# Conversions issued one operation at a time, the fold on one half of w_out at a time, and keys and queries loaded without a second copy

## The chip, the cores and the metric

The kernel runs on one core of one Trainium2 chip. The metric is the time of one execution on the device in microseconds (us). Three runs of the kernel before took 1641.61, 1646.22 and 1648.20 us, so the median is 1646.22. Five engines work side by side: TensorE (PE in the profile; its weight loads are shown as PEld), VectorE (DVE), ScalarE (ACT), GpSimd (POOL) and SyncE (SP), which here issues every DMA.

## The reference

The reference is an attention block followed by a gated network, all in float32; the network's weights arrive as float64.

```
scores = scale * q @ k^T                       # 8 batches, 12 heads, 448 rows, head size 64
scores = einsum('bhij,hg->bgij', scores, w_pre)  # mixes the 12 heads
attn   = softmax(scores - max)                 # over the 448 keys
attn   = einsum('bhij,hg->bgij', attn, w_post)
x      = attn @ v, written as 3584 tokens of 768
out    = ((x @ w1) * (x @ w2)) @ w3 @ w_out    # 768 -> 1024 -> 1024 -> 768
```

## The kernel before, in words

**Precision.** A float32 product is made of three faster products: each operand is split into a high part and a low part, and high x high, high x low and low x high are summed in one PSUM bank. The splitting is a CAST on ACT (or DVE) for the high part and a subtraction on POOL (or DVE) for the low part.

**Steps.** The attention is cut into 360 steps of ten query rows (45 per batch), each with all 12 heads. The loop in `run` writes the instructions of all engines step by step, and each engine works through its list in order; no scheduler moves anything. For step n the list holds: the fetch of the raw scores of step n+4 (`r`), the exponential with its minimum (`softmax(n)`: `mn` on DVE, `e` on ACT), the row sums and scaled weights of step n-1 (`scale`: `sa`, `ri`, `w` on DVE), the split of the scores of step n+2 (`split_r`: `rh`, `rl`), the product with `w_post` for step n-2 (`post`: `pso` on PE, copied to `mt` on ACT), and at the end the mix by `w_pre` of step n+1 (`mix`: three matmuls into `psm`). Every 15 steps come the products with v (`av`: `psa`, 48 matmuls in two of the steps). A mix is the mark of a step's end in what follows.

**Raw scores.** The raw scores of a batch go to DRAM (`raw_d`) before they are fetched in blocks of ten rows. For batch 0 they are made in full float32 from `kqz` (`qk_first`, `psz`): two heads at a time, one on the upper 64 rows of the array, one on the lower 64. For batches 1 to 7 they are made by `qk`, one unit per head and quarter of the rows, 7 x 48 = 336 units. The head's 64 rows of queries sit twice in a 128-row tile, and the keys' high part and low part share one 128-row tile `kk`. One matmul with the queries' high part (L193) gives high x high + high x low, and one with the low part (L194) gives the rest. Both contract over 128 rows. `load_kq` brings a pair of heads as three blocks of 448 columns: each head's queries twice over the partitions, and the keys once. `split_kq` makes `qh`, `ql` and `kk` from them.

**Weights.** Each float64 weight is read as two int32 words and made float32 by a conversion: a square on ACT (`cm`, L102) and four DVE operations (`ca` three times, `cx` once, L112 to L116) for a piece of up to 384 columns; then the piece is split. 40 pieces belong to w3 and w_out: `folding` multiplies w3 and w_out into one matrix w34 ahead of time (`psf`, L352), 384 matmuls in all, called atoms here. It walks over eight columns f of w3 and two halves of w_out. 32 pieces belong to w1 and w2. Before step 50 (`SWITCH`) the background work of TensorE is the fold; afterwards it is the network (`eg`, `eo` for batch 0, `e..` for the other batches in pairs, with seven products in place of eight). How many background atoms a step gets is set by a table `share`, which gives more to steps with less other matmul work. A step takes one whole piece, if there is one and the step has no product with v.

Of the kernel before, what the change touches and what calls it, by code (L numbers as in the profile page):

```python
# [17 lines left out]
HP = H // 2  # L18
# [27 lines left out]
class Kernel:  # L46
# [52 lines left out]
    def square(self, s, name):  # L99
        n = s.shape[1]  # L100
        m = self.cx.tile([128, CW], F32, tag="m", name=f"cm{name}", bufs=1)[:, :n]
        self.nc.scalar.activation(m, s[:, :, 1].bitcast(F32), AF.Square)  # L102
        return m

    def to_f32(self, s, m, name):


        nc, n = self.nc, s.shape[1]
        low, top = s[:, :, 0], s[:, :, 1]

        a = self.bank(5, f"ca{name}").bitcast(I32)[:, :n]
        nc.vector.tensor_scalar(a, top, 3, 0x3FFFFFFF, op0=ALU.logical_shift_left, op1=ALU.bitwise_and)  # L112
        nc.vector.scalar_tensor_tensor(a, top, -0x40000000, a, op0=ALU.bitwise_and, op1=ALU.bitwise_or)
        nc.vector.scalar_tensor_tensor(a, low, 29, a, op0=ALU.logical_shift_right, op1=ALU.bitwise_or)
        x = self.cx.tile([128, CW], F32, tag="x", name=f"cx{name}")[:, :n]
        nc.vector.scalar_tensor_tensor(x, m, TINY2, a.bitcast(F32), op0=ALU.is_ge, op1=ALU.mult)  # L116
        return x
# [5 lines left out]

    def converting(self, jobs):

        words, made = [], None
        jobs = list(jobs)
        for n in range(-2, len(jobs) + 1):  # L130
            if n + 2 < len(jobs):
                src = jobs[n + 2][0]
                words.append(self.words(src, f"{self.n_words}"))
                self.n_words += 1
            if made:
                jobs[n - 1][1](made)
                made = None
            if 0 <= n < len(jobs):
                s = words.pop(0)
                m = self.square(s, f"{self.n_made}")  # L140
            yield
            if 0 <= n < len(jobs):
                made = self.to_f32(s, m, f"{self.n_made}")
                self.n_made += 1
            yield
# [24 lines left out]
    def load_kq(self, b, p):  # L170
        t = self.kp.tile([128, 3, S], F32, tag="kq", name=f"kq{b}_{p}")
        self.nc.sync.dma_start(t, self.kq[b, p])
        self.kqs[b, p] = t

    def split_kq(self, b, h, q_lo, k_lo):
        nc, t, s = self.nc, self.kqs[b, h // 2], h % 2
        qh = self.kp.tile([128, S], F32R, tag="qh", name=f"qh{b}_{h}")
        ql = self.kp.tile([128, S], F32R, tag="ql", name=f"ql{b}_{h}")
        kk = self.kp.tile([128, S], F32R, tag="kk", name=f"kk{b}_{h}")
        a, z = slice(s * D, (s + 1) * D), slice((1 - s) * D, (2 - s) * D)  # L180
        nc.scalar.copy(qh, t[:, s])  # L181
        nc.scalar.copy(kk[a], t[a, 2])
        q_lo.tensor_tensor(ql, t[:, s], qh.bitcast(F32), op=ALU.subtract)  # L183
        k_lo.tensor_tensor(kk[z], t[a, 2], kk[a].bitcast(F32), op=ALU.subtract)
        self.parts[b, h] = (qh, ql, kk)

    def qk(self, b, h, c, i, copy):
# [6 lines left out]
        nc.tensor.matmul(p, ql[:, cols], kk, start=False, stop=True)  # L194
# [126 lines left out]
    def fold_jobs(self):  # L321
# [4 lines left out]
        yield from columns[0]  # L326
        for q in range(2):
            for k in range(KF):
# [3 lines left out]
        for f in range(1, KF):  # L332
            yield from columns[f]
# [6 lines left out]
    def folding(self):  # L340
        nc = self.nc
        for f in range(KF):
            for half in range(2):
                w = self.fw[f]

                i = 1 if f == half == 0 else 6 + half
                p = self.bank(i, f"psf{half}_{f}")[:, :DH]
                atoms = [(k, t, x, y) for k in range(KF) for t, (x, y) in enumerate(PAIRS)]
                for k, t, x, y in atoms:
                    if (k, t) != (0, 0):  # L350
                        yield
                    nc.tensor.matmul(p, w[:, k, x], self.fo[:, k, y, half * DH:(half + 1) * DH],  # L352
                                     start=(k == 0 and t == 0), stop=(k == KF - 1 and t == 2))
                z = self.fp.tile([128, 3, 2, 128], F32R, tag="z", name=f"fz{half}_{f}")
                q = p.rearrange("p (d c) -> p d c", c=128)
                dst = self.w34_d[half * 3:(half + 1) * 3, :, f].rearrange("d p t c -> p d (t c)")

                def low(z=z, q=q, dst=dst):
                    nc.vector.tensor_tensor(z[:, :, 1], q, z[:, :, 0].bitcast(F32), op=ALU.subtract)
                    self.later.append(lambda: nc.sync.dma_start(dst, z.rearrange("p d t c -> p d (t c)").bitcast(F32)))  # L360

                self.ends.append((i, lambda z=z, q=q: nc.scalar.copy(z[:, :, 0], q)))
                self.soon.append((i, low))
                yield
# [368 lines left out]
    def run(self):  # L733
# [20 lines left out]
        self.cs, self.n_words, self.n_made = self.pool("cs", 2), 0, 0  # L754
# [16 lines left out]
        fold_pieces = self.converting(self.fold_jobs())  # L771
        next(fold_pieces)
        next(fold_pieces)
        next(fold_pieces)
        next(fold_pieces)
# [10 lines left out]
        next(fold_pieces)  # L786
        next(fold_pieces)
# [26 lines left out]
        FOLD, SWITCH, E_AT = 18, NB + 5, NB + 8  # L814
# [34 lines left out]
        def there(p):  # L849

            f, r = divmod(p - 3 - 2 * KF, 3)
            return 2 * KF * 3 * (1 + f) + (0, 9, 18)[r] if f >= 0 else min(max(3 * (p - 3), 0), KF * 3)

        wanted, LF, turn = 0, 4, itertools.chain((6, 7, 0) * 9, itertools.cycle((6, 7)))
# [8 lines left out]
        next(fold_pieces)  # L863
        next(fold_pieces)
        held()
        next(fold_pieces)
        next(fold_pieces)
# [7 lines left out]
        self.unit_list = self.units()  # L875
        self.n_one, self.w_made = len(self.unit_list), 4 * KF
        self.unit_list += self.pair_units()
        unit_pieces, phases = self.converting(self.unit_jobs()), list(self.phases())
        nq, n_pieces = 0, -2
        for n in range(N + 6):  # L880
# [4 lines left out]
            if n == SWITCH:  # L885
# [5 lines left out]
                assert not fold_pieces  # L891
# [9 lines left out]
            if n == PAIR:  # L901

                assert done >= 2 * E_1 + E_2 and unit_pieces is None and not self.jobs and not self.ys
# [22 lines left out]

            p, pieces = self.n_made - 1 if fold_pieces else 2 * KF + 3 * KF, None
            if avs.get(n):
                pass
            elif fold_pieces:  # L930
                f = (self.n_made - 1 - 2 * KF) // 3
                if f < 2 or done >= 2 * KF * 3 * (f - 1):
                    pieces = fold_pieces
                    if next(pieces, self) is self:
                        fold_pieces = pieces = None
# [9 lines left out]
            for x in qks.get(n, []):  # L945
                store = self.qk(*x, nq % 2, nc.scalar.copy)
                nq += 1
                if store:
# [97 lines left out]
```

## Time and profile before

| | |
|---|---|
| three runs, median | 1641.61 to 1648.20 us, 1646.22 us |
| the profiled execution, its span | 1641.97 us, 1640.2 us |
| PE busy, DVE busy, ACT busy, POOL busy | 96%, 63%, 61%, 67% of the span |
| DMA | 446.10 MB, mean 272 GB/s |
| raw-score units (L193 and L194) | 336 pairs of matmuls |
| split of queries and keys (L181 to L184) | 84 of each |

The rows of the groups give the line, the engine, the operation, what is written from what, how many there are, the busy time and the mean duration of one, then the idle time of the engine just before them. A matmul row has the rows and columns of the array that it uses (128*112 is 128 rows by 112 columns). Matmuls overlap with the next one, so a matmul's duration is longer than the distance between two starts; the distance between starts is what a matmul takes of the engine.

### The profile page before, as it was taken

What the parts mean: (1) busy time and instruction counts of PE and PEld (TensorE: products, weight loads), DVE (VectorE), ACT (ScalarE), POOL (GpSimd) and SP (SyncE); (2) the same over time, 40 slices, a digit from 0 to 9 for tenths busy, and PEclk for the clock granted to TensorE, in tenths of its full rate; (3) what the DMA queues carried; (4) which work ended last, traced back from release to release, by engine and by line L of the source; (5) the groups of instructions that cost most, each with busy time, mean ns of one, the idle gap of its engine ahead of it and who ended that gap; (6) DMA issues with size and microseconds to landing.
All of it is one profiled execution on the core that took longest, in us unless ns stands there. A gap on an engine that the chain in (4) does not pass through costs nothing. (4 is left out here: it accounts for less than half of the span.)

```text
span 1640.2 us, 31803 instructions
## 1 busy us (share of the span) xinstructions
PE 1580.9 (96%) x10548; PEld 1419.6 (87%) x10548; DVE 1037.3 (63%) x2304; ACT 996.3 (61%) x2413; POOL 1098.8 (67%) x940
## 2 busy tenths in 40 slices
PE   6979999999999999999999999999999999999999
PEld 2569997888898888889899898899899898999988
DVE  5957767788757777863465565745555557634573
ACT  4867666677766676776666666666665554542321
POOL 3766555676657788884676776876675666655774
PEclk7989999999999999999999999999999999999999
DMA  8989779998899999999978977889988866779875
GB/s 264 320 258 284 240 238 295 286 310 274 277 268 305 317 335 329 323 345 304 318 242 268 294 242 238 260 269 304 308 254 245 241 190 195 215 220 308 284 234 180
DMA packets 233906, 446.10 MB, mean 272 GB/s; under 512 B 21838, under 2 KB 159054, under 8 KB 233678
## 3 DMA queue, kind: packets, MB, share of 16 engines
q1 hardware_dynamic: 233742, 444.08, 85.5%
q8 instruction: 83, 1.36, 0.4%
q14 instruction: 81, 0.66, 0.1%
HBM read 309.90 MB, written 134.09 MB: 271 GB/s over the span
## 5 line engine op out<-in xcount | busy, mean ns | idle before, releaser
L221 POOL TENSOR_TENSOR rl<-r,rh 120x448 fp32r<-120x448 f32 x360 | 447.4, 1243 | 326.5 <-DVE rh L220 108.6
L237 DVE TENSOR_REDUCE mn<-psm 120x1 f32<-120x448 f32 x360 | 223.9, 622 | 405.0 <-PE psm L230 403.7
L240 ACT ACTIVATE e<-psm,mn 120x448 f32<-120x448 f32 x360 | 228.0, 633 | 346.9 <-DVE sa L249 295.2
L263 PEld LDWEIGHTS pso<-w,e 120*112 120x112 f32 (+1 forms) x2880 | 346.3, 177 | 47.2 <-ACT mt L269 33.8
L263 PE MATMUL pso<-w,e 120*112 120x120 f32 (+1 forms) x2880 | 359.7, 268 | 18.9 <-ACT mt L269 18.5
L694 PE MATMUL e<-eh,wu 128*128 128x448 f32 x1008 | 304.0, 371 | 1.1 <-DVE c L648 1.1
L269 ACT COPY mt<-pso 112x480 f32<-112x480 f32 x360 | 206.6, 574 | 13.3 <-PE pso L263 8.5
L694 PEld LDWEIGHTS e<-eh,wu 128*128 128x128 f32 x1008 | 187.3, 188 | 15.6 <-DVE c L648 1.9
L220 DVE CAST rh<-r 120x448 fp32r<-120x448 f32 x342 | 193.9, 567 | 7.5 <-DMA r<-raw_d 7.1
L198 ACT COPY st<-psq 112x448 f32<-112x448 f32 x336 | 173.0, 526 | 30.4 <-DMA raw_d<-st 26.1
L694 PE MATMUL e<-el,wu 128*128 128x448 f32 x504 | 187.2, 372 | 2.4 <-POOL el L633 2.2
L294 PE MATMUL psa<-mt,v 112*64 112x150 f32 (+1 forms) x2304 | 157.5, 293 | 1.9 <-DMA v<-v 1.9
L183 POOL TENSOR_TENSOR ql<-kq,qh 128x448 fp32r<-128x448 f32 x84 | 98.7, 1175 | 80.3 <-ACT qh L181 79.9
L294 PEld LDWEIGHTS psa<-mt,v 112*64 112x64 f32 x2304 | 144.2, 137 | 8.3 <-DMA v<-v 2.3
L228 PE MATMUL psm<-rh,wph 120*120 120x448 f32 x360 | 139.1, 386 | 9.2 <-DVE rh L220 9.2
L648 DVE TENSOR_TENSOR c<-c,e 128x448 f32<-128x448 f32 x168 | 101.2, 615 | 68.4 <-PE e L694 64.1
L230 PE MATMUL psm<-rl,wph 120*120 120x448 f32 x360 | 132.6, 368 | 0.6 <-POOL rl L221 0.5
L229 PE MATMUL psm<-rh,wpl 120*120 120x448 f32 x360 | 132.4, 368 | 0.0
L193 PE MATMUL psq<-kk,qh 128*112 128x448 f32 x336 | 124.8, 372 | 7.7 <-ACT st L198 7.5
L514 PE MATMUL eg<-xh,wu 128*128 128x448 f32 x384 | 128.1, 383 | 0.0
L194 PE MATMUL psq<-kk,ql 128*112 128x448 f32 x336 | 123.2, 367 | 0.0
L633 POOL TENSOR_TENSOR el<-x,eh 128x448 fp32r<-128x448 f32 x90 | 105.6, 1194 | 9.1 <-DMA x<-x_d 5.4
(113 smaller groups left out, 2958.8 us busy)
## 6 DMA issues: line engine op xcount, KB each, us to landing
r<-raw_d SPq DMA_DIRECT2D x352, 210.0 KB, 4.3
raw_d<-st SPq DMA_DIRECT2D x168, 392.0 KB, 4.8
wu<-w_d SPq DMA_DIRECT2D x104, 384.0 KB, 5.7
wu<-s_d SPq DMA_DIRECT2D x96, 384.0 KB, 4.4
v<-v SPq DMA_DIRECT2D x144, 224.0 KB, 4.9
kq<-kq SPq DMA_DIRECT2D x42, 672.0 KB, 7.1
wu<-w_d SPq DMA_DIRECT2D x51, 512.0 KB, 5.9
wu<-s_d SPq DMA_DIRECT2D x36, 512.0 KB, 4.4
```

The costliest lines, as they stand in the source:

```text
L198: copy(st[:, c % 2], p)
L220: (nc.gpsimd if 1 < n < SCORES else nc.vector).tensor_copy(rh[:K], r[:K])
L221: nc.gpsimd.tensor_tensor(rl[:K], r[:K], rh[:K].bitcast(F32), op=ALU.subtract)
L228: nc.tensor.matmul(p[:K, :S], self.wph[:K, :K], rh[:K], start=True, stop=False)
L229: nc.tensor.matmul(p[:K, :S], self.wpl[:K, :K], rh[:K], start=False, stop=False)
L230: nc.tensor.matmul(p[:K, :S], self.wph[:K, :K], rl[:K], start=False, stop=True)
L237: nc.vector.tensor_reduce(mn[:K], p[:K, :S], axis=AX.X, op=ALU.min)
L240: nc.scalar.activation(e[:K], p[:K, :S], AF.Exp, bias=mn[:K], scale=-1.0, accum_out=sm[:K])
L263: nc.tensor.matmul(p[:, j, :, :w], e[:K, j * JT:(j + 1) * JT], w2[:K, :, :w], start=True, stop=True)
L269: self.ends.append((4, lambda: copy(dst, p[:, :, :, :w])))
L294: nc.tensor.matmul(self.psa[rows, g % 3, :W], v[:, j, rows], mt[:, j, 2 * g + s, :W], start=(j == 0), stop=(j == NJ - 1))
L694: nc.tensor.matmul(p, w[:, k, x], ops[m, k][y], start=(k == 0 and t == 0), stop=(k == nk - 1 and t == 2))
```

## The change

**Keys and queries.** `load_kq` loads two blocks of 448 columns: the queries of both heads over the 128 partitions, and the keys. `split_kq` writes the queries' high part into both halves of its tile by two CASTs of 64 rows (before: one of 128 rows), and the low part only into the head's own 64 rows. The second matmul of a unit contracts over those 64 rows alone. It leaves out low x low, a term that the first version added. The `kq` tile has three buffers (before: two, of three blocks).

**Conversions.** One queue of 72 pieces replaces the two generators. A step issues DVE operations of it one at a time: two per step before step 20, four from there to step 56, then three and four in turn; none in a step that has products with v, and a piece is not begun just ahead of such a step.

**The fold.** The pieces come as column 0 of w3, the first half of w_out, column 1, the second half, and then columns 2 to 7. The groups of atoms run as (column 0, half 0), (1, 0), (0, 1), (1, 1), and then as before. `FOLD`, `SWITCH` and `E_AT` go from 18, 50 and 53 to 20, 57 and 59. The atoms of a step are at most 18 and bounded by the pieces that are there (`there`).

**Raw-score units.** In a step with two units, the second one comes after `post` and `av` (before: both ahead of the background atoms).

```
-        t = self.kp.tile([128, 3, S], F32, tag="kq", name=f"kq{b}_{p}")
+        t = self.kp.tile([128, 2, S], F32, tag="kq", name=f"kq{b}_{p}", bufs=3)
...
-        nc.scalar.copy(qh, t[:, s])
-        nc.scalar.copy(kk[a], t[a, 2])
-        q_lo.tensor_tensor(ql, t[:, s], qh.bitcast(F32), op=ALU.subtract)
-        k_lo.tensor_tensor(kk[z], t[a, 2], kk[a].bitcast(F32), op=ALU.subtract)
+        nc.scalar.copy(qh[a], t[a, 0])
+        nc.scalar.copy(kk[a], t[a, 1])
+        nc.scalar.copy(qh[z], t[a, 0])
+        q_lo.tensor_tensor(ql[a], t[a, 0], qh[a].bitcast(F32), op=ALU.subtract)
+        k_lo.tensor_tensor(kk[z], t[a, 1], kk[a].bitcast(F32), op=ALU.subtract)
...
         nc.tensor.matmul(p, qh[:, cols], kk, start=True, stop=False)
-        nc.tensor.matmul(p, ql[:, cols], kk, start=False, stop=True)
+        a = slice(h % 2 * D, (h % 2 + 1) * D)
+        nc.tensor.matmul(p, ql[a, cols], kk[a], start=False, stop=True)
...
-        yield from columns[0]
         for q in range(2):
+            yield from columns[q]
             for k in range(KF):
...
-        for f in range(1, KF):
+        for f in range(2, KF):
             yield from columns[f]
...
+        order = [(0, 0), (1, 0), (0, 1), (1, 1)] + [(f, half) for f in range(2, KF) for half in range(2)]
+        for n, (f, half) in enumerate(order):
...
-        FOLD, SWITCH, E_AT = 18, NB + 5, NB + 8
+        FOLD, SWITCH, E_AT = 20, NB + 12, NB + 14
...
-            for x in qks.get(n, []):
-                store = self.qk(*x, nq % 2, nc.scalar.copy)
+            qk(qks.get(n, [])[:1])
...
-            if pieces:
-                next(pieces)
+            left, free = 2 if n < FOLD else 4 if n < SWITCH else 3 + n % 2, not avs.get(n + 1)
+            while not avs.get(n) and self.c_words and (left > 0 or self.c_op and not free):
...
+                self.convert()
+                left -= 1
...
             if n < SWITCH:
-                wanted += now
-                now = max(min(there(p), KF * 3 + wanted) - done, 0)
+                now = min(spread(n, SWITCH - 1, total), 18) if n >= FOLD else 0
+                now = min(there(p), max(done + now, KF * 3 * 3)) - done
+            elif n < LATE:
+                now = min(3 * K1 // 2 * (p - n_fold) - done, spread(n, LATE, E_1))
...
             for x in avs.get(n, []):
                 self.av(*x)
+            qk(qks.get(n, [])[1:])
```

The first place is TensorE between the mixes of steps 27 and 28. `psq` is a raw-score unit, `psf` the fold, `pso` the product with `w_post`. Before:

```order
L228 MATMUL psm_1844<-rh_1742,wph 120x448
L229 MATMUL psm_1844<-rh_1742,wpl 120x448
L230 MATMUL psm_1844<-rl_1743,wph 120x448
L193 MATMUL psq_7_0_1884<-kk_7_1719,qh_7_1717 112x448
L194 MATMUL psq_7_0_1884<-kk_7_1719,ql_7_1718 112x448
L193 MATMUL psq_7_1_1889<-kk_7_1719,qh_7_1717 112x448
L194 MATMUL psq_7_1_1889<-kk_7_1719,ql_7_1718 112x448
L352 MATMUL psf_2_1836<-fo,fw_1520 128x384 x6
L263 MATMUL pso_1905<-w_1801,e_1733 112x120 x4
L352 MATMUL psf_2_1836<-fo,fw_1520 128x384 x6
```

The same stretch in the changed kernel (L196 and L198 are now the two matmuls of a unit, L357 the fold, L267 `pso`):

```order
L232 MATMUL psm_1645<-rh_1561,wph 120x448
L233 MATMUL psm_1645<-rh_1561,wpl 120x448
L234 MATMUL psm_1645<-rl_1562,wph 120x448
L196 MATMUL psq_7_0_1682<-kk_7_1540,qh_7_1538 112x448
L198 MATMUL psq_7_0_1682<-kk_7_1540,ql_7_1539 112x448
L357 MATMUL psf_0_1579<-fo,fw_212 128x384
L267 MATMUL pso_1696<-w_1612,e_1552 112x120 x4
L196 MATMUL psq_7_1_1701<-kk_7_1540,qh_7_1538 112x448
L198 MATMUL psq_7_1_1701<-kk_7_1540,ql_7_1539 112x448
L357 MATMUL psf_0_1579<-fo,fw_212 128x384 x2
```

The step has 3 atoms of the fold where it had 12, its second unit stands behind `pso`, and each unit ends in a matmul (L198) that uses 64 rows of the array, which the row does not show.

The second place is DVE from the minimum of step 6 to that of step 8. Before, each step has a whole piece:

```order
L237 TENSOR_REDUCE mn_560<-psm_543 120x1
L249 TENSOR_SCALAR sa_565<-sm_503 120x1
L250 RECIPROCAL ri_566<-sa_565 120x1
L253 TENSOR_SCALAR w_567<-wpo,ri_566 120x120
L112 TENSOR_SCALAR ca_582<-cs_444 128x384
L113 SCALAR_TENSOR_TENSOR ca_582<-cs_444,ca_582 128x384
L114 SCALAR_TENSOR_TENSOR ca_582<-cs_444,ca_582 128x384
L116 SCALAR_TENSOR_TENSOR cx_586<-cm_558,ca_582 128x384
L237 TENSOR_REDUCE mn_610<-psm_596 120x1
```

And now:

```order
L241 TENSOR_REDUCE mn_516<-psm_501 120x1
L253 TENSOR_SCALAR sa_521<-sm_464 120x1
L254 RECIPROCAL ri_522<-sa_521 120x1
L257 TENSOR_SCALAR w_523<-wpo,ri_522 120x120
L131 TENSOR_SCALAR ca_540<-cs_356 128x384
L133 SCALAR_TENSOR_TENSOR ca_540<-cs_356,ca_540 128x384
L241 TENSOR_REDUCE mn_556<-psm_548 120x1
L253 TENSOR_SCALAR sa_561<-sm_519 120x1
L254 RECIPROCAL ri_562<-sa_561 120x1
L257 TENSOR_SCALAR w_563<-wpo,ri_562 120x120
L135 SCALAR_TENSOR_TENSOR ca_540<-cs_356,ca_540 128x384
L138 SCALAR_TENSOR_TENSOR cx_579<-cm_514,ca_540 128x384
```

A piece now takes two steps in this stretch.

More of the change, by code (lines that the diff above doesn't have):

```diff
@@ L97, in words, with ask_words @@
         return s
[L99 to L117, printed above, removed]
+    def ask_words(self):
+        if self.c_asked < len(self.c_jobs):
+            self.c_words.append(self.words(self.c_jobs[self.c_asked][0], f"{self.c_asked}"))
+            self.c_asked += 1
@@ L341, in folding @@
         nc = self.nc
[L342 to L364, printed above, removed]
@@ L770, in run, with piece @@
         nc.sync.dma_start(self.wpo, self.wpost)
[L771 to L775, printed above, removed]
+        self.unit_list = self.units()
+        self.n_one, self.w_made = len(self.unit_list), 4 * KF
+        self.c_jobs, self.c_words, self.c_square, self.c_made = [*self.fold_jobs(), *self.unit_jobs()], [], None, None
+        self.c_asked = self.c_piece = self.c_op = self.c_parts = 0
+        n_fold = 2 * KF + 3 * KF
+        self.ask_words()
+        self.ask_words()
+        def piece():
+            self.begin_conversion()
+            for _ in range(4):
+                self.convert()
         nc.vector.tensor_scalar_mul(wsc, w, -0.125)
```

150 lines of the change are left out of this document (91 added, 59 removed).

## The prediction

> **What bounds the kernel now.** I read the page first, then the span cut at chosen mixes into stretches of equal make-up, then the waits, and last the order in time of TensorE's instructions, because a matmul's duration says less than the distance between two starts.
>
> ```profile
> span 1640.2 us, 31803 instructions
> PE 1580.9 (96%) x10548; PEld 1419.6 (87%) x10548; DVE 1037.3 (63%) x2304; ACT 996.3 (61%) x2413; POOL 1098.8 (67%) x940
> ...
> L193 PE MATMUL psq<-kk,qh 128*112 128x448 f32 x336 | 124.8, 372 | 7.7 <-ACT st L198 7.5
> ...
> L194 PE MATMUL psq<-kk,ql 128*112 128x448 f32 x336 | 123.2, 367 | 0.0
> ```
>
> ```profile
> core 0: us, PE busy (x) PEld busy (x) DVE busy (x) ACT busy (x) POOL busy (x), PEclk, DMA share, GB/s
> ...
> 21.10:97.70 76.60, 66.39 (x286) 38.70 (x287) 59.61 (x131) 54.79 (x130) 50.79 (x56) 0.85 0.94 307
> 97.70:123.20 25.50, 22.05 (x185) 20.00 (x183) 14.40 (x34) 15.40 (x37) 17.13 (x17) 0.93 0.78 242
> 123.20:169.20 46.00, 44.79 (x276) 42.42 (x275) 37.01 (x90) 33.85 (x83) 29.09 (x27) 1.00 0.90 280
> 169.20:179.00 9.80, 9.80 (x91) 9.22 (x89) 6.86 (x17) 5.45 (x14) 5.49 (x6) 1.00 0.85 256
> 179.00:280.40 101.40, 97.36 (x685) 89.96 (x684) 73.17 (x188) 64.23 (x153) 56.04 (x51) 1.00 0.82 252
> 280.40:296.60 16.20, 16.20 (x97) 14.17 (x97) 14.94 (x41) 13.04 (x33) 12.29 (x11) 1.00 0.99 328
> 296.60:467.50 170.90, 161.98 (x1175) 143.68 (x1173) 131.42 (x334) 118.06 (x281) 115.31 (x103) 1.00 0.90 282
> 467.50:530.10 62.60, 62.38 (x435) 56.99 (x434) 40.43 (x86) 41.07 (x103) 40.69 (x30) 1.00 0.95 293
> 530.10:1449.20 919.10, 905.91 (x6317) 830.14 (x6317) 553.62 (x1228) 593.34 (x1475) 655.25 (x541) 1.00 0.86 273
> ```
>
> From 123 us on TensorE is busy for nearly all of each stretch, so what is added to its work there is added to the time, less what its own idle time takes in: 4.0 us in 179 to 280, 8.9 in 297 to 468, 13.2 in 530 to 1449. Only the stretch from 21 to 98 us is different: TensorE idles 10.2 of 76.6 us, its granted clock is 0.85, and the DMA engines are busy for 0.94 of it at 307 GB/s. There transfers set the pace.
>
> **The second matmul of a unit, 336 times.** The second matmul still streams 448 columns and loads 112 columns of weights. What is new is that the array is used in two shapes in turn: 128 rows for L193, 64 for its partner, 128 or so for whatever follows. The trace holds such turns. First ordinary neighbours, without one:
>
> ```profile
> 148.20 0.36 PE L194 MATMUL psq<-kk,ql 128*112 128x448 f32 x1
> 148.40 1.21 PE L352 MATMUL psf<-fo,fw 128*128 128x384 f32 x6
> 149.45 0.98 PE L263 MATMUL pso<-w,e 120*112 120x120 f32 x8
> ```
>
> A matmul of 448 columns takes 0.20 (148.20 to 148.40), one of the fold's 384 columns 1.05/6 = 0.175. Now the 64-row pairs of batch 0 inside a busy stretch (x4: two pairs side by side, two passes each):
>
> ```profile
> 53.80 0.37 PE L229 MATMUL psm<-rh,wpl 120*120 120x448 f32 x1
> 54.01 0.36 PE L230 MATMUL psm<-rl,wph 120*120 120x448 f32 x1
> 54.30 1.01 PE L158 MATMUL psz<-kqz 64*112 64x448 f32 x4
> 55.24 0.45 PE L352 MATMUL psf<-fo,fw 128*128 128x384 f32 x1
> 55.52 0.98 PE L263 MATMUL pso<-w,e 120*112 120x120 f32 x8
> ```
>
> Into the 64-row shape, L230 to L158 is 0.29 where 0.20 is usual: 0.09 lost. Out of it, the fold's single matmul L352 is 0.28 ahead of the next, where 0.175 is usual: 0.105 lost. Between, the two passes take 0.94. How long passes of this kind last undisturbed is seen in runs of them (the time of a run ends with the last one's own duration, of which the page has the mean):
>
> ```profile
> L263 PE MATMUL pso<-w,e 120*112 120x120 f32 (+1 forms) x2880 | 359.7, 268 | 18.9 <-ACT mt L269 18.5
> ...
> L294 PE MATMUL psa<-mt,v 112*64 112x150 f32 (+1 forms) x2304 | 157.5, 293 | 1.9 <-DMA v<-v 1.9
> ```
>
> ```profile
> 175.02 0.78 PE L263 MATMUL pso<-w,e 120*112 120x120 f32 x6
> ```
>
> ```profile
> 176.14 2.34 PE L294 MATMUL psa<-mt,v 112*64 112x150 f32 x34
> ```
>
> 120 columns: (0.78 - 0.27)/5 = 0.103; so 448 columns take 0.385, two passes 0.77, and 0.17 is lost inside. The whole visit costs 0.09 + 0.17 + 0.105 = 0.37 us. The other change of shape, to 64 columns in `psa`, in pairs side by side of (2.34 - 0.29)/16 = 0.128 each, says the same:
>
> ```profile
> 174.92 0.98 PE L263 MATMUL pso<-w,e 120*112 120x120 f32 x8
> 175.83 3.28 PE L294 MATMUL psa<-mt,v 112*64 112x150 f32 x48
> 179.04 0.47 PE L228 MATMUL psm<-rh,wph 120*120 120x448 f32 x1
> 179.35 0.37 PE L229 MATMUL psm<-rh,wpl 120*120 120x448 f32 x1
> ```
>
> 24 pairs are 3.07 and take 3.21 (0.14 lost); L263 to L294 is 0.91 for 8 x 0.103 = 0.82 (0.09 lost); behind them L228 to L229 is 0.31 for 0.20 (0.10 lost): 0.33 for one visit. I read both as a pause of 0.09 at each change while the array runs empty, and a first weight load of some 0.1 after each, which is not laid under the matmul ahead as the others are. A unit is one visit of a single matmul, so it pays all four parts: **0.37 us**. Bounds: 0.33 (`psa`) to 0.38 (rounded starts); below, 0.18, if only the pauses are paid; nothing at all is a rival.
>
> [...]
>
> Where the units lie, counted in the new order of TensorE by mixes: 10 in 21 to 98, 7 up to 123, 19 up to 169, 3 up to 179, 29 up to 280, 5 up to 297, 49 up to 468, 18 up to 530, 196 up to 1449.
>
> **The background work, moved.** Fold atoms in those first stretches: 24, 27, 125, 14, 194 before; 21, 3, 42, 6, 312 now. Network matmuls: 23, 31, 234 before in the stretches from 179, 280 and 297; 0, 21, 267 now. An atom is 0.175, a network matmul 0.20. What TensorE is spared early it must do after 179.
>
> **The conversions.** Nine fewer pieces are asked for by step 17 (13 instead of 22), and the loads of keys and queries shrink by a third.
>
> ```profile
> kq<-kq SPq DMA_DIRECT2D x42, 672.0 KB, 7.1
> ...
> cs<-wo SPq DMA_DIRECT2D x16, 384.0 KB, 6.9
> ```
>
> ```profile
> ACT cm L102 <- DMA cs<-wo: 11.2, 7, 4.4
> ...
> PE psz L158 <- ACT sz L163: 5.9, 5, 3.4
> ```
>
> So up to 98 us there are 9 x 393 KB + 3 x 229 KB + one stored result of 393 KB = 4.6 MB less to move; at 307 GB/s that is 15 us. The waits of that stretch show the same cause: ACT stands behind words that have not landed, and TensorE behind ACT. TensorE's idle time there is 10.2. I take **-10**, bounds 0 (latency remains) and -15. The ten units there pay 3.7 on TensorE, under the transfers.
>
> **Between 123 and 169** the spared atoms give nothing to speak of, because DVE is next. Ten steps, ten pieces now (nine before):
>
> ```profile
> L237 DVE TENSOR_REDUCE mn<-psm 120x1 f32<-120x448 f32 x10 | 6.2, 620 | 7.9 <-PE psm L230 7.9
> L253 DVE TENSOR_SCALAR w<-wpo,ri 120x120 f32<-120x120 f32 x10 | 5.7, 568 | 0.3
> L113 DVE SCALAR_TENSOR_TENSOR ca<-cs,ca 128x384 int32<-128x384 int32 (+1 forms) x9 | 4.7, 518 | 0.3
> L220 DVE CAST rh<-r 120x448 fp32r<-120x448 f32 x10 | 4.4, 439 | 0.0
> ```
>
> A step with a piece is 4 x 0.52 + 0.62 + 0.57 + 0.44 and 0.3 for two small ones, 4.0, and about 0.25 of gaps between nine instructions: 4.3 against 4.6 now. TensorE falls from 44.8 by 83 x 0.175 = 14.5 and rises by 19 x 0.37 = 7.0 to 37.3, below that. So -3, bounds 0 and -7.
>
> **The extra CAST** of a head is 84 x about 0.57 us of ACT over the span, with ACT busy 61%; it lies beside TensorE's matmuls. POOL's subtraction keeps its 448 columns. Fewer bytes after 98 us gain nothing where TensorE is the bound. If that cover were gone, the CAST would cost up to 48 us; ACT is at 593 of 919 us in the long stretch, so it is not.
>
> **The sum**, in us against the span of 1640.2:
> - 21 to 98: -10.
> - 98 to 123: atoms -24 x 0.175 = -4.2, units 7 x 0.37 = +2.6, one to two of its idle 3.5: -3.
> - 123 to 169: -3. To 179: -1.4 + 1.1 = 0.
> - 179 to 280: +118 x 0.175 = +20.7, -23 x 0.20 = -4.6, units +10.7, idle -2: +25.
> - 280 to 297: -2 + 1.9 = 0 (DVE is as busy as before, 14.9 of 16.2).
> - 297 to 468: +33 x 0.20 = +6.6, units 49 x 0.37 = +18.1, and 6 of the 8.9 idle, since pieces come evenly: +19.
> - 468 to 530: units +6.7: +7.
> - 530 to 1449: 196 x 0.37 = +72.5, half of the 13.2 idle: +66.
> - Behind 1449: nothing.
>
> Together +101: a span of 1741, and with the 1.8 us around the span in the profiled execution (1641.97) **1743 us**. The median shown, 1646.2, is 4 us above that execution, so a median may lie as much higher.
>
> **The rivals.**
> 1. *Only the pauses are paid* (0.18 a unit), the first weight load being laid under as elsewhere. For it: a single matmul leaves half of the array free. Against: L352 behind the pairs. From 179 on 297 units save 0.19 each, 56 us: 1687. [...]
> 2. *The 64 rows cost nothing*, being one group in one bank with the matmul ahead; then the change is faster. The place is 21 to 98 us, the price the 15 us of transfers, and it decides if a unit keeps its 0.40. Sum without the units: -15, -5, -3, -1, +14 (179 to 280), -2, +1, 0: -11, so 1631. Atoms put off under a DVE bound give part of the early gain back; with an early gain of only 10 it is 1636. Against: no turn in the trace is free.
> 3. *A cold start*: with fewer atoms TensorE idles more before 98 us and stays at a low clock.
>
> ```profile
> 20.00:40.00 20.00, 16.82 (x43) 7.60 (x43) 11.81 (x25) 9.02 (x22) 10.42 (x12) 0.55 0.94 290
> 40.00:60.00 20.00, 19.63 (x109) 12.81 (x107) 18.36 (x43) 15.65 (x37) 12.97 (x16) 1.00 0.95 307
> ```
>
> Its 66.4 us at a clock of 0.85 are 56 at full clock and 103 at 0.55: 26 more than the stretch takes now. Half of that, +13 in place of -10, gives 1766. Against it: full clock from 40 us on.
>
> **How the numbers follow.** Forecast 77%, own range 1722 to 1765 (0.33 to 0.38 a unit is -12 to +3, the early stretch -5 to +10, the idle time +14); pauses only 9%, free 9%, cold 5%. The range of 1680 to 1768 takes in most of the pauses-only case and leaves the free case and half of the cold one out. About 0.5%, 8 us, is what a measurement of this kernel tells from no change. The free case splits into 5% faster (under 1634) and 4% the same; the rest, 91%, is slower.
>
> **What would show it.** In the changed profile L196 to L198 starts 0.29 apart and L198 to its successor as much, with another 0.1 behind that one; the stretch with the last 196 units grows by some 65 us; 21 to 98 shrinks by about 10 with fewer GB; DVE, not TensorE, is nearly full between 115 and 155. Distances of 0.20 at L198 would make the prediction wrong, and so would an early stretch as long as before.

## The result, and the profile after

The changed kernel takes 1742.8 us (median of four runs, 1736.4 to 1748.3) against 1644.8 us (four runs, 1641.6 to 1648.2): a ratio of 1.059, with a 95% interval of 1.056 to 1.061. It is slower, by 98 us; the forecast was 1743. All ratios below are to the kernel before, which was run again beside each group of experiments: its medians there are 1645.1 to 1646.7 us, so a difference between kernels of two groups is uncertain by 1 to 2 us.

The page of the changed kernel, with the rows that answer to those of L193 and L194:

```profile
span 1734.6 us, 31883 instructions
...
PE 1695.2 (98%) x10548; PEld 1398.5 (81%) x10548; DVE 1024.7 (59%) x2304; ACT 1054.0 (61%) x2497; POOL 1097.4 (63%) x940
...
L198 PE MATMUL psq<-kk,ql 64*112 64x448 f32 x336 | 153.9, 458 | 0.0
...
L198 PEld LDWEIGHTS psq<-kk,ql 64*112 64x112 f32 x336 | 57.3, 170 | 103.0 <-issue 103.0
...
L196 PE MATMUL psq<-kk,qh 128*112 128x448 f32 x336 | 127.7, 380 | 4.2 <-ACT st L202 2.8
```

TensorE has the same number of matmuls (10548) and is busy for 114 us more. DVE and POOL do no more than before; ACT is busy for 58 us more, with 84 more CASTs. L198 waits for nothing, yet its mean duration is 458 ns where L194's was 367. The row of its weight loads says where to look: 103 us of idle time on the loading side, 0.31 us for each of 336, released by nothing but the engine itself.

The span cut at the same mixes as before (the same nine stretches, columns as in the prediction):

```profile
core 0: us, PE busy (x) PEld busy (x) DVE busy (x) ACT busy (x) POOL busy (x), PEclk, DMA share, GB/s
21.40:95.80 74.40, 67.72 (x284) 38.37 (x284) 40.34 (x98) 51.25 (x119) 44.73 (x50) 0.82 0.87 282
95.80:116.10 20.30, 19.03 (x159) 14.23 (x158) 9.80 (x25) 13.83 (x33) 14.01 (x14) 1.00 0.63 186
116.10:158.30 42.20, 38.26 (x192) 26.94 (x192) 36.64 (x87) 33.53 (x79) 28.23 (x27) 1.00 0.83 269
158.30:169.80 11.50, 10.15 (x84) 7.76 (x83) 7.22 (x16) 7.31 (x19) 7.51 (x7) 1.00 0.71 216
169.80:293.20 123.40, 122.31 (x780) 105.19 (x779) 83.91 (x212) 76.71 (x177) 60.83 (x56) 1.00 0.73 217
293.20:313.50 20.30, 16.95 (x88) 13.04 (x87) 18.01 (x44) 13.76 (x33) 11.97 (x11) 0.92 0.77 229
313.50:497.10 183.60, 183.27 (x1208) 147.22 (x1206) 139.89 (x351) 130.59 (x302) 120.07 (x107) 1.00 0.88 275
497.10:565.70 68.60, 68.60 (x435) 55.69 (x434) 40.72 (x86) 45.02 (x109) 41.11 (x31) 1.00 0.88 269
565.70:1543.60 977.90, 974.83 (x6318) 815.72 (x6317) 542.54 (x1228) 625.27 (x1521) 652.13 (x540) 1.00 0.80 250
```

Set against the rows of before, and against a kernel of the experiments below that has the new schedule with the old keys and queries ("schedule alone"), the stretches change by (us):

| stretch before | forecast | changed kernel | schedule alone |
|---|---|---|---|
| 0 to 21 | 0 | +0.3 | -0.6 |
| 21 to 98 | -10 | -2.2 | -8.7 |
| 98 to 123 | -3 | -5.2 | -4.3 |
| 123 to 169 | -3 | -3.8 | -2.4 |
| 169 to 179 | 0 | +1.7 | +2.1 |
| 179 to 280 | +25 | +22.0 | +15.2 |
| 280 to 297 | 0 | +4.1 | +3.1 |
| 297 to 468 | +19 | +12.7 | +11.0 |
| 468 to 530 | +7 | +6.0 | +0.2 |
| 530 to 1449 | +66 | +58.8 | +1.2 |
| behind | 0 | 0.0 | -0.1 |
| span | +101 | +94.4 | +16.7 |

The profiled executions do not all lie at the median of their runs: that of before is 3 to 5 us below it, that of the changed kernel 6.4 us below (it had the highest granted clock of its four runs, 0.989, where the others had 0.980 to 0.984), that of the schedule alone at it. So the span of the changed kernel grows by 3.6 us less than the median (94.4 for 98.0), and that of the schedule alone by 5 us more (16.7 for 11.6).

TensorE's order in time in the long stretch of the changed kernel shows one unit:

```profile
802.11 0.36 PE L234 MATMUL psm<-rl,wph 120*120 120x448 f32 x1
802.31 0.37 PE L196 MATMUL psq<-kk,qh 128*112 128x448 f32 x1
802.61 0.46 PE L198 MATMUL psq<-kk,ql 64*112 64x448 f32 x1
803.00 0.47 PE L550 MATMUL eo<-el,wu 128*128 128x448 f32 x1
803.30 0.57 PE L550 MATMUL eo<-eh,wu 128*128 128x448 f32 x2
```

L234 to L196 is 0.20, as before the change. L196 to L198 is 0.30, L198 to L550 is 0.39, and L550 to the next is 0.30. Over the 293 units that start between 180 and 1500 us the medians are 0.293, 0.385 and 0.309 (0.309 where the successors have 448 columns); in the kernel before they are 0.204, 0.203 and 0.203. A unit costs 0.09 + 0.18 + 0.11 us more, 0.378 before rounding.

The weight loads of the same unit show where a part of it comes from:

```profile
802.61 0.17 PEld L198 LDWEIGHTS psq<-kk,ql 64*112 64x112 f32 x1 [0.32 <-issue]
...
803.00 0.19 PEld L550 LDWEIGHTS eo<-el,wu 128*128 128x128 f32 x1 [0.22 <-issue]
```

Before, the load of the second matmul started together with the first one's streaming (the first matmul, L193, starts at 800.17 too):

```profile
800.17 0.18 PEld L194 LDWEIGHTS psq<-kk,ql 128*112 128x112 f32 x1
```

In the changed kernel it starts 0.30 us after L196 (802.31), together with its own matmul, and the load behind it again starts only with its own matmul. Over all 336 units the load of the second matmul starts 0.29 us after the first matmul (median); before, 0.00. The load behind it starts 0.38 us after the second matmul and 0.00 ahead of its own (medians); before, 0.00 after and 0.20 ahead. So in these units the first load after each of the two changes of shape no longer lies under the matmul ahead.

### The profile page after: what moved, and what is told of

It is laid out like the page before. It is cut to its first block, busy times and chain, and to the rows that moved or that the text cites. A ratio compares the mean times of both kernels' runs of the same rounds, so it can differ in the third digit from the quotient of the medians.

```text
span 1734.6 us, 31883 instructions
## 1 busy us (share of the span) xinstructions
PE 1695.2 (98%) x10548; PEld 1398.5 (81%) x10548; DVE 1024.7 (59%) x2304; ACT 1054.0 (61%) x2497; POOL 1097.4 (63%) x940
## 5 line engine op out<-in xcount | busy, mean ns | idle before, releaser
L267 PEld LDWEIGHTS pso<-w,e 120*112 120x112 f32 (+1 forms) x2880 | 345.3, 177 | 37.0 <-ACT mt L273 12.4
L267 PE MATMUL pso<-w,e 120*112 120x120 f32 (+1 forms) x2880 | 361.0, 268 | 9.5 <-ACT mt L273 9.5
L699 PE MATMUL e<-eh,wu 128*128 128x448 f32 x1008 | 308.9, 376 | 0.1
L224 DVE CAST rh<-r 120x448 fp32r<-120x448 f32 x342 | 183.0, 535 | 3.6 <-DMA r<-raw_d 2.5
L186 POOL TENSOR_TENSOR ql<-kq,qh 64x448 fp32r<-64x448 f32 x84 | 97.2, 1158 | 106.2 <-ACT qh L183 95.3
L198 PE MATMUL psq<-kk,ql 64*112 64x448 f32 x336 | 153.9, 458 | 0.0
L198 PEld LDWEIGHTS psq<-kk,ql 64*112 64x112 f32 x336 | 57.3, 170 | 103.0 <-issue 103.0
L234 PE MATMUL psm<-rl,wph 120*120 120x448 f32 x360 | 132.7, 369 | 0.1
L196 PE MATMUL psq<-kk,qh 128*112 128x448 f32 x336 | 127.7, 380 | 4.2 <-ACT st L202 2.8
```

Source lines behind the costliest of these rows:

```text
L198: nc.tensor.matmul(p, ql[a, cols], kk[a], start=False, stop=True)
L224: (nc.gpsimd if 1 < n < SCORES else nc.vector).tensor_copy(rh[:K], r[:K])
L267: nc.tensor.matmul(p[:, j, :, :w], e[:K, j * JT:(j + 1) * JT], w2[:K, :, :w], start=True, stop=True)
L699: nc.tensor.matmul(p, w[:, k, x], ops[m, k][y], start=(k == 0 and t == 0), stop=(k == nk - 1 and t == 2))
```

## The experiments

**128 rows again, in the changed kernel.** The second matmul contracts over all 128 rows; the rows that hold no low part are zero, set once in two fixed tiles. Everything else of the change stays.

```
-        ql = self.kp.tile([128, S], F32R, tag="ql", name=f"ql{b}_{h}")
+        ql = self.qls[s]
...
-        a = slice(h % 2 * D, (h % 2 + 1) * D)
-        nc.tensor.matmul(p, ql[a, cols], kk[a], start=False, stop=True)
+        nc.tensor.matmul(p, ql[:, cols], kk, start=False, stop=True)
...
+        self.qls = [cp.tile([128, S], F32R, name=f"ql{s}") for s in range(2)]
+        for s in range(2):
+            nc.gpsimd.memset(self.qls[s].bitcast(F32)[(1 - s) * D:(2 - s) * D], 0.0)
```

> The changed kernel with one thing taken back: the second matmul of a unit contracts over 128 rows again. The low part lies in two fixed tiles whose other half is zero, so the sums are those of the changed kernel; loads, CASTs, conversions and fold stay as changed. Theory (the array changes its shape twice for each unit, 0.38 us by the starts in the changed kernel's trace): the distances of 0.29, 0.385 and 0.31 around the second matmul go back to 0.20, the stretch that holds the last 196 units falls from 978 to about 915 us, and the whole from 1743 to about 1645 (1635 to 1655), the kernel before. Rival (the schedule is the loss: fold atoms put off, pieces spread, the three CASTs of a head): the time stays above 1720.

Measured: 1659.7 us, 1.008 times the kernel before (1.006 to 1.010). Its TensorE in the long stretch:

```profile
802.00 0.36 PE L196 MATMUL psq<-kk,qh 128*112 128x448 f32 x1
802.20 0.37 PE L197 MATMUL psq<-kk,ql 128*112 128x448 f32 x1
802.40 0.37 PE L549 MATMUL eo<-el,wu 128*128 128x448 f32 x1
```

All distances are back to 0.20, and the time falls by 83 us (1742.8 - 1659.7) although the matmul now multiplies 64 rows of zeros. So the price hangs on the 64 rows. But 1659.7 is above the 1635 to 1655 that was expected: what is left of the change costs 13 us, where the sum without the units said that it would gain.

**Keys and queries alone.** The kernel before, with the loads, the split and the 64-row matmul of the change and nothing else of it.

```
-        t = self.kp.tile([128, 3, S], F32, tag="kq", name=f"kq{b}_{p}")
+        t = self.kp.tile([128, 2, S], F32, tag="kq", name=f"kq{b}_{p}", bufs=3)
...
+        a = slice(h % 2 * D, (h % 2 + 1) * D)
+        nc.tensor.matmul(p, ql[a, cols], kk[a], start=False, stop=True)
```

> The kernel before with the part on keys and queries alone: two blocks loaded, three CASTs, second matmul over 64 rows; conversions, fold and order as before. Theory: about 0.38 us for each unit from 123 us on, less what TensorE's idle time takes in: 1645 + 90, so 1735 (1725 to 1745). Rival (schedule): 1645, or less by the bytes spared.

Measured: 1733.7 us, ratio 1.052 (1.050 to 1.054), 87 us above the runs beside it (1646.7). From the other side, with the old schedule, the price is the same within 4 us. The kernel with the same loads and 128 rows, further down, takes 1649.0 us, so 85 of the 87 us hang on the 64 rows.

**The schedule alone.** The changed kernel, with `load_kq`, `split_kq` and `qk` as they were before (the two edits above, turned round).

> The changed kernel with keys and queries as before (three blocks, one CAST for the queries' high part, second matmul over 128 rows with low x low): what is left is the part on conversions, fold and order of the units. Theory: 1645 (1635 to 1655), since what the early stretches gain is given back between 179 and 300 us. Rival (schedule): 1720 or more.

Measured: 1658.3 us, ratio 1.006 (1.004 to 1.008). This agrees with the first experiment, has none of its fixed tiles and zeros, and like it lies above the 1635 to 1655 that was expected. The new schedule, without the 64 rows, is slower by 12 us. Its stretches that differ most from before:

```profile
20.50:88.40 67.90, 60.66 (x284) 36.80 (x285) 40.58 (x98) 48.45 (x114) 44.01 (x49) 0.86 0.92 304
...
165.10:281.70 116.60, 113.13 (x780) 108.45 (x778) 84.68 (x212) 71.99 (x170) 60.81 (x56) 0.99 0.78 237
281.70:301.00 19.30, 15.19 (x87) 13.73 (x87) 16.80 (x43) 12.21 (x30) 10.80 (x10) 0.91 0.76 231
301.00:482.90 181.90, 171.88 (x1210) 150.66 (x1208) 140.23 (x354) 124.24 (x291) 121.36 (x108) 0.99 0.90 285
```

The early gain is there, -8.7 us. The stretch from 165 us holds 780 matmuls where it held 685, and TensorE's busy time rises from 97.4 to 113.1: the work that was put off. From 301 on TensorE has 35 matmuls more than before (1210 for 1175) and idles 10 us, as much as before (8.9).

**The second matmul twice.** To tell a price per matmul from a price per visit, the 64-row matmul is issued twice in a row; the result then holds that product twice.

```
+        nc.tensor.matmul(p, ql[a, cols], kk[a], start=False, stop=False)
         nc.tensor.matmul(p, ql[a, cols], kk[a], start=False, stop=True)
```

> The changed kernel with the second matmul of each unit issued twice in a row (the low part's product is added twice; the output is off by that). It tells what is paid per visit to the 64-row shape and what per matmul. If the price is per visit, the twin starts some 0.20 us after the first one's streaming begins and adds about 0.20 x 297 = 59 us: 1802. If each 64-row matmul waits for its own weight load, 0.29 each: 1829. If each pays the whole 0.37 on top of its 0.20: 1910.

Measured: 1804.8 us, ratio 1.095 (1.093 to 1.098): 62 us more than the changed kernel, close to the 1802 of a price per visit. TensorE in its long stretch:

```profile
801.12 0.36 PE L196 MATMUL psq<-kk,qh 128*112 128x448 f32 x1
801.41 0.45 PE L198 MATMUL psq<-kk,ql 64*112 64x448 f32 x1
801.70 0.36 PE L199 MATMUL psq<-kk,ql 64*112 64x448 f32 x1
802.00 0.66 PE L520 MATMUL eg<-xh,wu 128*128 128x448 f32 x2
802.50 0.36 PE L520 MATMUL eg<-xl,wu 128*128 128x448 f32 x1
```

Four distances in a row are long by 0.09 to 0.11: into L198, L198 to its twin, the twin to the next, and the one behind it (medians 0.295, 0.294, 0.294, 0.309). Their sum is 1.192 for 4 x 0.203 = 0.812: 0.380 for the visit, the same as with one matmul. So each change of shape makes two gaps longer by 0.09 to 0.11 here, the one at the change and the one behind the first matmul of the new shape. With a single 64-row matmul the second of these and the next change fall into the same gap, which is why L198 is followed by 0.385.

**Loads once, nothing else.** The kernel before, with keys and queries loaded without a second copy, the split into two CASTs, and the second matmul over 128 rows with zeros as in the first experiment: the loads are a third smaller, and TensorE works as before.

```
-        t = self.kp.tile([128, 3, S], F32, tag="kq", name=f"kq{b}_{p}")
+        t = self.kp.tile([128, 2, S], F32, tag="kq", name=f"kq{b}_{p}", bufs=3)
...
+        ql = self.qls[s]
```

> The kernel before with keys and queries loaded once (two blocks, three CASTs), but the second matmul over 128 rows, its other half zero; conversions and fold as before. It tells what the spared bytes are worth without the change of shape. Theory: nothing that can be measured, since 9.6 MB less are moved mostly where TensorE is the bound: 1645 (1637 to 1652). Rival (bytes set the pace early, and 0.9 MB less by 100 us shorten it; or the CASTs cost): 1637 or less, or 1655 or more.

Measured: 1649.0 us, ratio 1.0015 (1.0002 to 1.0028). The 42 smaller loads and the extra CAST together gain nothing. What holds its ACT between 20 and 310 us, among the waits for DMAs:

```profile
ACT st L199 <- DMA raw_d<-st: 12.3, 8, 4.5
ACT cm L102 <- DMA cs<-wo: 6.1, 4, 4.1
```

**A third store buffer.** ACT copies the raw scores out of PSUM into `st`, of which there were two; it waits until the stores from an older `st` have landed, 12.3 us in the rows above. The room of the third key tile is given to a third `st`, in the kernel of the last experiment and in the one with 128 rows in the changed kernel.

```
-            st = (self.qp if p % 2 else self.kp).tile([JT, 2, S], F32, tag="st", name=f"sz{p}_{c}", bufs=2)
+            st = (self.qp if p % 2 else self.kp).tile([JT, 2, S], F32, tag="st", name=f"sz{p}_{c}", bufs=2 if p % 2 else 3)
...
-            self.st = self.kp.tile([JT, 2, S], F32, tag="st", name=f"st{b}_{h}_{c}")
+            self.st = self.kp.tile([JT, 2, S], F32, tag="st", name=f"st{b}_{h}_{c}", bufs=3)
...
-        t = self.kp.tile([128, 2, S], F32, tag="kq", name=f"kq{b}_{p}", bufs=3)
+        t = self.kp.tile([128, 2, S], F32, tag="kq", name=f"kq{b}_{p}")
```

> The same with a third buffer for the raw scores on their way to DRAM (st) in place of the third one for the loads of keys and queries. Theory (ACT stands behind a store that has not landed, and with it mt and TensorE): the stalls of the second matmul's place between 87 and 135 us (1.7, 3.5, 0.3 and 0.9 us in the kernel before) and the low clock behind two of them go: 5 to 9 us less than without, 1638. Rival (transfers are the bound there, the buffer only moves the wait): no difference.

> The changed kernel with 128 rows in the second matmul (1659.7 before this edit) and a third buffer for the stores of raw scores, one less for the loads of keys and queries. Theory (what is left of the loss, 13 us, is stalls behind stores that have not landed, 8.1 us at the unit's first matmul and some of the 12.0 at pso, and half clock behind them): 8 to 12 us less, 1650. Rival (the loss is the fold put off under a DVE bound): unchanged, 1660.

Measured: 1637.6 us, ratio 0.995 (0.993 to 0.997), on the old schedule, which is faster than both kernels; and 1648.2 us, ratio 1.001 (1.000 to 1.0025), on the new one. Both gain 11.4 us (from 1649.0 and 1659.7). In both the wait for `raw_d` is gone from ACT; what remains for DMAs on the old schedule between 20 and 310 us is

```profile
ACT cm L102 <- DMA cs<-wo: 6.3, 5, 4.4
...
ACT fz L363 <- DMA r<-raw_d: 0.5, 1, 0.5
```

In the kernel before that wait was larger than the one for the words of the weights (11.2 us), and in the schedule alone it was the largest of all. The two rows, first that of the kernel before:

```profile
ACT st L198 <- DMA raw_d<-st: 17.5, 11, 3.2
...
ACT st L200 <- DMA raw_d<-st: 19.5, 9, 4.7
```

So the store buffers are a bound of both schedules. How ACT's wait reaches TensorE is seen on the old one: there TensorE's wait for the copies into `st` falls from 10.0 to 3.9 us. On the new one it hardly falls (8.6 to 7.6), so how the 11.4 us come about is not shown there. The buffers are not what separates the two schedules: with three of them the new schedule is still 10.6 us behind the old one.

**A later first unit piece.** In the changed kernel the first piece of w1 and w2 is begun one step before the switch. Behind the switch ACT and TensorE then stall. The rows between 280 and 320 us of the kernel with 128 rows:

```profile
ACT wu L146 <- DVE ca L135: 3.9, 1, 3.9
...
PE pso L266 <- ACT mt L272: 4.1, 1, 4.1
```

ACT's CAST into `wu` waits 3.9 us, and TensorE's `pso` behind it 4.1. The row names DVE. My reading, from the order of the pools, was that the tile takes the room of the fold's last results and waits for their store to land. The experiment lets the first piece begin one step later (on top of the third store buffer).

```
-   room = i == n_fold and n == SWITCH - 1 or n >= SWITCH and 2 * done >= 3 * K1 * (i - n_fold - 4)
+   room = n >= SWITCH and 2 * done >= 3 * K1 * (i - n_fold - 4)
```

> The same, and the first piece of w1 and w2 is begun at step 57, not at 56, so that its CAST on ACT does not stand behind the last store of the fold, whose room it takes (a stall of 4.1 us at pso near 285 us). Theory: 3 to 5 us less than without, 1646. Rival: the stall moves to the next CAST, no difference.

Measured: 1646.2 us, ratio 0.9997 (0.9985 to 1.001). The same window of its waits:

```profile
PE eg L518 <- POOL wu L147: 1.4, 1, 1.4
PE pso L266 <- ACT mt L272: 1.0, 2, 0.6
```

The stall of 4.1 us is gone, a new one of 1.4 us stands at `eg`, and the stretch falls from 19.5 to 16.1 us. The median falls by 2.0 us, half of the stall and less than the 3 to 5 that were expected. That the early piece causes the stall is shown. That it waits for the store of the fold's results fits the traces: in the four that have the stall, the last of these stores lands 0.10 us before the CAST starts, while the tile `cx` that the CAST reads was finished 3.5 us earlier or more. The operation on DVE that the row names ends 0.01 to 0.02 us before it, but the CAST uses nothing of it.

**Four operations per step from step 10.** Since 8.6 us still lay between this kernel and the old schedule with the same buffers, the last two runs undo single edits of the new schedule, in whole or in part. For four operations per step from the very start there is no time: the instructions of that kernel block each other (a deadlock). In the first run, the conversions have four operations per step from step 10 on instead of from step 20.

```
-   left, free = 2 if n < FOLD else 4 if n < SWITCH else 3 + n % 2, not avs.get(n + 1)
+   left, free = 2 if n < 10 else 4 if n < SWITCH else 3 + n % 2, not avs.get(n + 1)
```

> As the kernel with a later first unit piece (1646.2 us), but with four operations of the conversions per step from step 10 instead of from step 20. Theory: what the schedule of the change still costs against the old schedule with the same buffers (1637.6) comes from the fold's matmuls that are put off because their pieces come late; ten steps with twice the operations are five pieces more by step 20, so some 60 to 80 of the fold's matmuls move ahead of 169 us and out of the stretch from 162 to 278 us, and the time falls by 3 to 7 us, to 1639 to 1643. Rival: VectorE sets the pace of these steps at four operations each, so the stretch from 98 to 169 us lengthens by as much as the later one shrinks, and the time stays at 1644 to 1649. Second rival: the rule on room holds the pieces back, and the number of fold matmuls in each stretch stays as it is: 1646 too.

Measured: 1640.3 us, ratio 0.997 (0.996 to 0.998), 5.9 us less than its base. The matmuls of the fold by stretch (columns as before without POOL; `psf` alone), first its base:

```profile
20.80:86.10 65.30, 6.92 (x21) 3.56 (x21) 0.00 (x0) 0.00 (x0) 0.88 0.95 306
86.10:110.30 24.20, 0.86 (x3) 0.56 (x3) 0.55 (x1) 0.51 (x1) 0.93 0.68 209
110.30:150.90 40.60, 10.25 (x42) 7.67 (x42) 0.54 (x1) 0.50 (x1) 1.00 0.84 269
150.90:162.40 11.50, 1.70 (x7) 1.05 (x6) 0.00 (x0) 0.00 (x0) 1.00 0.71 213
162.40:278.40 116.00, 63.93 (x314) 55.20 (x312) 7.11 (x13) 6.32 (x13) 0.99 0.77 227
```

and with the earlier operations:

```profile
20.20:89.90 69.70, 11.43 (x42) 7.37 (x42) 0.55 (x1) 0.51 (x1) 0.89 0.95 313
89.90:114.00 24.10, 3.11 (x13) 2.16 (x12) 0.55 (x1) 0.50 (x1) 0.93 0.76 238
114.00:153.50 39.50, 11.96 (x53) 9.25 (x51) 0.83 (x2) 1.00 (x2) 1.00 0.81 251
153.50:163.50 10.00, 2.16 (x11) 1.55 (x9) 0.26 (x1) 0.00 (x0) 1.00 0.90 288
163.50:270.40 106.90, 55.24 (x270) 47.34 (x270) 6.02 (x11) 5.80 (x12) 1.00 0.77 231
```

44 atoms leave the last of these stretches (314 to 270), fewer than the 60 to 80 expected, and 21, 10, 11 and 4 are added ahead of it. The first stretch grows by 4.4 us; its DMA engines are busy for 0.95 of it in both kernels. The stretches between give back 2.7 us, and the last falls by 9.1: more than 44 x 0.175 = 7.7. The same atoms cost less early, where TensorE has idle time (1.7 us in the four stretches together), than late, where it is nearly full (9.1). The spans of these two executions differ by 8.1 us, the medians by 5.9.

**Both units ahead.** In the second, both raw-score units of a step stand ahead of the background work again.

```
-            qk(qks.get(n, [])[:1])
+            qk(qks.get(n, []))
...
-            qk(qks.get(n, [])[1:])
```

> The same kernel (1646.2 us) with both raw-score units of a step ahead of the background work, as in the kernel before, instead of the second one behind post and av. Theory: the place of the second unit is neutral, since its results are wanted much later and TensorE is busy either way: 1644 to 1649. Rival: two units in a row need two PSUM banks and two copies at once, so that TensorE waits for the copies again, and putting the second one later saved that: 1650 to 1655.

Measured: 1646.1 us, ratio 1.000 (0.999 to 1.001), the same as its base (1646.2). The place of the second unit is neutral.

## Why the prediction was right, and where it was not

**The price of a unit: right.** 0.378 us measured for 0.37 summed from batch 0's pairs, in the parts 0.09, 0.18 and 0.11 for 0.09, 0.17 and 0.105. The reading had two parts. Of the first, a pause while the array runs empty, the traces show the length, 0.09 us, and not what the array does in it. The second, a first weight load that is not laid under the matmul ahead, is seen in the loads of L198 and L550, which start 0.00 us ahead of their own matmuls. That the price hangs on the change of shape and is paid per visit is shown by the two kernels with and without it (83 and 87 us) and by the twin, whose visit costs 0.380. The prediction's list of signs put L198 to its successor at 0.29, "as much" as L196 to L198; that was wrong (0.385), though the sum had counted 0.09 and 0.17 for the two.

**What the units cost in all: mis-sized.** By 336 x 0.378 it would be 127 us; 83 to 87 were paid. The term that was too small is the idle time that takes units in. In the long stretch the forecast was +66, made of 72.5 for the units less 6.6 (half of the 13.2 idle); the growth is 58.8. Set each distance between two starts to the median of its kind (the same two matmuls behind the same third one): the stretch then adds up to 898.0 us before and 970.5 after, +72.5 as forecast. What the distances exceed these medians by falls from 21.1 to 7.4 us, so 13.7 were taken in and not 6.6. The idle time of the rows falls by less (13.2 to 3.1), because a row counts a wait only from the end of the matmul ahead, and a matmul's duration is longer than its distance to the next (0.36 for 0.20). Between 297 and 468 the units found almost all the idle time (8.9 to 0.3); the kernel with 128 rows keeps 8.3 there and is only 5.4 us shorter, for 49 x 0.378 = 18.5.

**21 to 98: -10 forecast, -2.2 measured.** The schedule alone gives -8.7, so the step about the transfers is nearly right: what moved fell by 2.9 MB there (76.6 us at 307 GB/s to 67.9 at 304), not by 4.6. The changed kernel lost the rest, and not to the transfers. Its late part, in slices of 20 us:

```profile
60.00:80.00 20.00, 17.43 (x82) 9.62 (x80) 11.36 (x29) 14.78 (x34) 13.11 (x14) 1.00 0.94 317
80.00:100.00 20.00, 18.27 (x79) 12.05 (x81) 6.04 (x16) 14.45 (x33) 12.19 (x14) 0.74 0.49 156
```

and TensorE's order in time at the seam:

```profile
78.17 0.36 PE L234 MATMUL psm<-rl,wph 120*120 120x448 f32 x1
81.33 1.01 PE L160 MATMUL psz<-kqz 64*112 64x448 f32 x4 [2.80 <-ACT st L202]
```

TensorE stands still for 2.8 us behind ACT, which waits 4.2 us at that point for a store from `st` to land, and the granted clock is 0.74 in the 20 us after, with the DMA engines half idle. This is not the third rival, a cold start for want of fold atoms: from 20 to 40 us the clock is 0.55 in both kernels, and between 80 and 100 us it is 0.83 in the kernel before and 0.75 in the one with keys and queries alone, which have the old fold. Nor do the units show in it: with 128 rows the stretch is 6.1 us shorter, but the next one is 5.9 us longer (26.2 for 20.3, at a clock of 0.87). Where such a stall falls moves several us between neighbouring stretches. From 21 to 179 as a whole, the forecast was -16, the changed kernel has -9.5, the one with 128 rows -11.7 and the schedule alone -13.3. By the prediction's own list, an early stretch as long as before would have made it wrong, and 74.4 for 76.6 comes near to that. Another sign did not come at all: between 116 and 158 us DVE is busy for 36.6 of 42.2 us, less than TensorE (38.3).

**The schedule: wrong in sign.** The sum without the units (the second rival's) was -11; the two kernels without the units' price are 13 and 12 us slower than before. The step of the moved work was right: 179 to 280 was to grow by 14 without the units and grew by 15.2. From 98 to 179 it gave -4.6 for a forecast of -9. Three others were further out. 21 to 98 stood at -15 in that sum and gave -8.7. 280 to 297 stood at -2 and gave +3.1, with a stall behind the piece that is begun one step before the switch. And 297 to 468 stood at +1, because its idle time was to shrink by 6 "since pieces come evenly"; without the units it did not shrink at all (10.0 us idle for 8.9), and the moved network matmuls (33 x 0.20 = 6.6) came on top; these two are 7.7 of the +11.0, and the rest is not settled. With three store buffers the new schedule is 10.6 us behind the old one: the early piece is 2.0 of it, the conversions that come forward from step 10 on are 5.9, and 2.7 stay open.

**The total was right partly because two errors cancel.** Forecast: units +112 and the rest -11. Measured: units +83 to +87, the rest +12 to +13. Each miss is some 25 us. That the kernel would be slower was safe, since the price of the units is many times the rest. That the median was hit within 1 us was luck: the span, which the sum was made for, is 6 us below its forecast (1734.6 for 1741).

**The rivals.** Only pauses paid (1687) falls with the distances behind L198 (0.385 and 0.309). The free case (1631 to 1636) falls with the same, and its own sum falls too, since a kernel with no price on the units is at 1658 to 1660.

## What to carry to other kernels

In this kernel a matmul over half the rows between matmuls over all of them was no saving but a loss, 0.378 us a visit and 83 to 87 us in all: look at the distances between starts around each change of array shape, and if they are longer, pad with zeros (83 us less here) or put the visits together (two matmuls in one visit lost 0.380, no more than one). Bytes and conversions spared early were worth less than the idle time that the bound engine had there (8.7 us gained by the schedule alone, for 10.2 idle before); what was put off with them was paid nearly in full where that engine had little idle time (the stretch from 179 to 280 us grew by 15.2 us, its matmuls by 15.8). And before a schedule is changed, look at which buffers wait for their stores to land: a third one was worth as much here as all that the schedule lost (11.4 us for 11.6).

## What the runs showed that was not expected

- Each change of array shape between 128 and 64 rows lengthened two gaps between starts by some 0.09 us (0.11 where the next matmul loads 128 columns of weights, 0.088 where `pso` follows with 112): the gap at the change and the one after the first matmul in the new shape. Where a single matmul stands in the new shape, as L198 does, the second delay of one change and the first of the next add up in one gap (0.385 for 0.203).
- The loading side shows it directly: the weight loads of L198 idle 0.31 us each with nothing to wait for (103.0 us for 336), because they start only with their own matmul, 0.29 us after L196.
- The stores of 392 KB of raw scores held ACT up early for longer than the loads of the weights' words: between 20 and 310 us, 17.5 us for 11.2 in the kernel before and 19.5 for 4.3 in the schedule alone. In the two kernels with three store buffers this wait is gone. The prediction had looked only at the words.
